# A router fed by a DMA transpose of float16 halves, with broadcast routing instructions, in a fused attention and mixture-of-experts kernel

## The chip, the cores and the metric

The program runs on one core of a Trainium2 chip. The metric is the device time of one execution in microseconds. Names of engines: PE is TensorE (PEld is its weight load), DVE is VectorE, ACT is ScalarE, POOL is GpSimd, SP is SyncE, which here only issues DMAs. "Lnnn" is a line of the kernel before, unless a text says that it is a line of the changed one.

## The reference, cut to what matters

Three layers follow one another on 2304 tokens: attention that keeps the 32 largest scores of each row, a gated two-layer network, and a mixture of eight experts in which a router picks two experts for every token.

```python
def _moe2_ref(x, w_gate, w_noise, noise, w1, w2):
    logits = x @ w_gate                                   # x: 2304 x 512, w_gate: 512 x 8
    noise_scale = np.log1p(np.exp(x @ w_noise))
    noisy_logits = logits + noise_scale * noise
    top2 = np.argpartition(-noisy_logits, 2, axis=1)[:, :2]
    top2_l = np.take_along_axis(noisy_logits, top2, axis=1)
    top2_l = top2_l - top2_l.max(-1, keepdims=True)
    top2_w = np.exp(top2_l)
    top2_w /= top2_w.sum(-1, keepdims=True) + 1e-09
    for e in range(E):
        for k in range(2):
            mask = top2[:, k] == e
            h = np.maximum(x[mask] @ w1[e], 0.0)
            out[mask] += top2_w[mask, k, None] * (h @ w2[e])
```

The router's choice is a comparison of close numbers, so its product is held to about float32. Large matmuls run on pairs of float16 numbers (a high half and the rest, a low half), as three products: high by high, high by low, low by high.

## The kernel before, in words

**The work and its stages.** Attention goes through 80 units (a pair of heads by 128 or 64 query rows). Four heads' pairs of the same rows fill a chunk of 128 or 256 tokens; there are 12 chunks, 18 tiles of 128 tokens. When a chunk is filled, `moe1` runs the gated network on it, then the router, and enters every token in the table of its two experts by an indirect DMA. When all chunks are entered, `expert` reads the tables, gathers the tokens' rows from `xd` in DRAM, turns them by a DMA transpose (L790) and runs the experts' two layers. So attention, the gated network and routing overlap from about 190 to 920 us, and experts alone follow.

**What sets the order.** Nothing is ordered by the hardware: every engine runs its instructions in the order of the program. The class `Plan` makes that order: each piece of work is an `op` with an engine, an assumed duration, a priority, the ops that it follows, an assumed delay until they see its result, and counted buffers (`alloc` takes one, the last `use` gives it back). `Plan.run` plays this through and emits every op at its turn. PE's order, DMA issues on SP, all of it comes out of that, so an edit of one op can move everything behind it. Buffers that matter here: `tp`, three PSUM banks; `y`, four SBUF tiles of 128x584 float32, used by attention's masked scores and by the router.

**The router's steps for one tile**, in `moe1`. Six ops `wo` (L573) sum the network's second layer in PSUM. `ev` on ACT copies it to `x2` (L582) and its high half to `xs` (L585). `xlo` on POOL makes the low half (L588). `xout` on SP writes both halves to `xd` (L593). Beside that, `rt` on PE turns the float32 `x2` by four transposes into a `tp` bank (L612), `re` on ACT copies that to a `y` tile (L616), and four ops `rl` multiply it with the router's weights `wr`, in float32 (L619; the profile shows two matmuls for each). For a chunk, `r1` on ACT takes exp and log (L630, L631), `r2` on DVE finds the two largest and marks them, expert by expert, one instruction for each tile and choice (L647), `r3` on PE counts the tokens ahead (L656 to L659), `r4` on DVE turns that into places, one instruction for each tile and choice (L675), and `r5` on POOL scatters (L681).

**The end.** `counts` (L844 on) counts the tokens of each expert and how many blocks overflow; a table of thresholds for it is made by an iota on POOL when it is needed (L869). In these inputs the fallback `layers(False)` and `overflow` are not run.

```python
                for kb in range(4):
                    P.transpose(q.ps[:, kb, :], ch.x2[t][:, kb * 128:(kb + 1) * 128], ident)        # rt, PE
...
                A.activation(q.xt, q.ps, AF.Copy)                                                   # re, ACT
...
                P.matmul(q.lg[:, t, 0:16], q.xt[:, kb, :], wr[:, kb, :], start=kb == 0, stop=kb == 3)  # rl, PE
```

Of the kernel before, what the change touches and what calls it, by code (L numbers as in the profile page):

```python
# [29 lines left out]
SPROD = 2.0 * SX * SV  # L30
NEG = -1.0e30
# [6 lines left out]
SW = S + 8  # L38
# [89 lines left out]
def attention_moe_kernel(ctx: ExitStack, tc: tile.TileContext, qT, kT, v, w_gate, w_val, w_out,  # L128
# [34 lines left out]
    nbi = const.tile([1, E + 2], I32, name="nbi")  # L163
    ohsum = const.tile([128, E], FH, name="ohsum")
# [15 lines left out]
    def layers(fast):  # L180
# [335 lines left out]
        def moe1(ch, prio):  # L516
# [43 lines left out]
            ch.x2, ch.hx2 = [], []  # L560
            evs = []
            for t in range(nt):
# [17 lines left out]
                def ev(r=r, t=t):  # L580
                    x2 = tile_of("x2", [128, DM], FT)
                    A.activation(x2, r.ps, AF.Copy, scale=SX2 / (SPROD * SO))  # L582
                    ch.x2.append(x2)
# [3 lines left out]
                def xlo(r=r, t=t):  # L587
                    G.tensor_tensor(r.xs[:, DM:], ch.x2[t], r.xs[:, :DM], op=OP.subtract)  # L588
# [7 lines left out]
                a = op("POOL", 1.25, prio - 1000, xlo, [evs[-1]], use=[hx, hxs])  # L596
                written.append(op("SP", 1.0, prio - 2000, xout, [a], use=[hxs], lat=3.0))
                ch.hx2.append(hx)
# [5 lines left out]
            for t in R:  # L604
                hp_, hr = plan.tile("tp"), plan.tile("y")

                def rt(t=t):
                    if t == 0:
                        q.lg = tile_of("tp", [128, nt, 32], FT)
                    q.ps = tile_of("tp", [128, 4, 128], FT)  # L610
# [3 lines left out]
                def re(t=t):  # L614
                    q.xt = tile_of("y", [128, SW], FT)[:, :512].rearrange("p (k f) -> p k f", k=4)
                    A.activation(q.xt, q.ps, AF.Copy)  # L616

                def rl(kb, t=t):
                    return lambda: P.matmul(q.lg[:, t, 0:16], q.xt[:, kb, :], wr[:, kb, :], start=kb == 0, stop=kb == 3)  # L619
                a = op("PE", 0.44, prio - 2000, rt, [evs[t]] + dep, alloc=([hl] if t == 0 else []) + [hp_], use=[ch.hx2[t]],  # L620
                       chain="moe")
                b = op("ACT", 0.5, prio - 2000, re, [a], alloc=[hr], use=[hp_])

                dep = [b]
                for kb in range(4):
                    dep = [op("PE", 0.06, prio - 2000, rl(kb), dep, use=[hr, hl], lat=0.15 if kb < 3 else None, dma=kb < 3)]
# [432 lines left out]
```

## Time and profile before

| | |
|---|---|
| median of 3 runs | 1322.95 us (1322.31 to 1325.13) |
| the profiled execution | 1323.6 us, its span 1321.9 us |
| PE busy | 1228.2 us, 93% of the span |
| PEld busy | 896.4 us, 68% |
| DVE busy | 869.1 us, 66% |
| ACT busy | 791.6 us, 60% |
| POOL busy | 740.9 us, 56% |
| mean granted clock of PE | 0.955 of 2.4 GHz |
| DMA | 119.93 MB, 91 GB/s over the span |

The shares are means over stages: weights and attention until about 190 us, attention with the gated network and routing until about 900 us, experts until the end. A busy PE is counted from the start of a matmul to its modelled end, and matmuls overlap; what one costs PE is therefore read from the distance of two starts, not from its length.

### The profile page before, as it was taken

What the parts mean: (1) busy time and instruction counts of PE and PEld (TensorE: products, weight loads), DVE (VectorE), ACT (ScalarE), POOL (GpSimd) and SP (SyncE); (2) the same over time, 40 slices, a digit from 0 to 9 for tenths busy, and PEclk for the clock granted to TensorE, in tenths of its full rate; (3) what the DMA queues carried; (4) which work ended last, traced back from release to release, by engine and by line L of the source; (5) the groups of instructions that cost most, each with busy time, mean ns of one, the idle gap of its engine ahead of it and who ended that gap; (6) DMA issues with size and microseconds to landing.
All of it is one profiled execution on the core that took longest, in us unless ns stands there. A gap on an engine that the chain in (4) does not pass through costs nothing. (4 is left out here: it accounts for less than half of the span.)

```text
span 1321.9 us, 29643 instructions
## 1 busy us (share of the span) xinstructions
PE 1228.2 (93%) x10669; PEld 896.4 (68%) x10670; DVE 869.1 (66%) x3608; ACT 791.6 (60%) x1788; POOL 740.9 (56%) x1005
## 2 busy tenths in 40 slices
PE   5578799799999999999999999999999999999997
PEld 3347466586776867886777876877666666676674
DVE  6999889998799887888789875455114324233111
ACT  5777678787777877786787774565224324333221
POOL 5989887787476786666676654442222322222221
PEclk9558899899999899999999999999999999999999
DMA  7434331342004310014100003167547576575441
GB/s 222 115 108 122 124 106 27 100 133 112 17 2 101 87 47 10 11 36 121 53 2 2 18 9 97 50 185 204 99 73 194 122 159 171 102 189 132 77 72 22
DMA packets 104463, 119.93 MB, mean 91 GB/s; under 512 B 56561, under 2 KB 65905, under 8 KB 104306
## 3 DMA queue, kind: packets, MB, share of 16 engines
q1 hardware_dynamic: 94194, 97.97, 27.1%
q0 software_dynamic: 10112, 19.97, 8.2%
q8 instruction: 86, 1.41, 0.5%
q14 instruction: 71, 0.58, 0.2%
HBM read 77.22 MB, written 20.63 MB: 74 GB/s over the span
## 5 line engine op out<-in xcount | busy, mean ns | idle before, releaser
L534 PEld LDWEIGHTS <-w 128*128 128x128 f16 x3456 | 276.9, 100 | 38.0 <-issue 12.9
L534 PE MATMUL mm<-xch,w 128*128 128x256 f16 (+1 forms) x2880 | 285.9, 256 | 7.4 <-ACT th L541 3.7
L812 DVE SCALAR_TENSOR_TENSOR g<-mm,g 128x256 f16<-128x256 f32 (+1 forms) x192 | 72.0, 379 | 243.6 <-ACT g L809 233.1
L402 POOL TENSOR_TENSOR y<-sS,sg 128x576 f32<-128x576 f32 x144 | 194.9, 1354 | 9.1
L804 PE MATMUL mm<-xch,w 128*128 128x256 f16 (+1 forms) x2016 | 190.3, 255 | 0.0
L804 PEld LDWEIGHTS <-w 128*128 128x128 f16 x2016 | 170.2, 98 | 23.5
L361 DVE MAX8 cand<-sS 128x8 f32<-128x72 f32 x1152 | 166.8, 217 | 20.6 <-ACT sS L352 20.2
L830 PEld LDWEIGHTS <-g 128*128 128x128 f16 x960 | 92.8, 98 | 106.3 <-DVE g L812 3.4
L573 PE MATMUL mm<-w,g 128*128 128x512 f16 x648 | 158.2, 389 | 1.0 <-POOL w L281 0.7
L424 DVE SCALAR_TENSOR_TENSOR e<-sS,good,e 128x576 f32<-128x576 f32 x144 | 155.5, 1099 | 2.3 <-ACT e L379 1.5
L786 POOL DMA_INDIRECT v<-xd,ids x40 | 47.0, 1175 | 163.5 <-DVE ws L776 155.1
L842 POOL DMA_INDIRECT out<-e,ids x40 | 63.8, 1595 | 131.3 <-ACT e L839 58.6
L809 ACT ACTIVATE g<-mm 128x256 f16<-128x256 f32 (+1 forms) x192 | 65.8, 346 | 112.6 <-PE mm L804 106.6
L551 POOL TENSOR_TENSOR g<-th,g 128x128 f16<-128x128 f32 (+1 forms) x144 | 93.5, 653 | 68.8 <-ACT g L548 65.7
L409 DVE MAX8 good<-y 128x8 f32<-128x584 f32 x144 | 109.9, 763 | 25.8 <-POOL y L402 21.0
L396 ACT ACTIVATE sg<-sS,m 128x576 bf16<-128x576 f32 x144 | 110.7, 770 | 23.5 <-POOL m L387 22.6
L494 PE MATMUL tp<-pt,v 128*64 128x128 f32 (+3 forms) x1600 | 116.9, 285 | 7.0 <-ACT e L379 5.1
L830 PE MATMUL tp<-w,g 128*128 128x512 f16 x504 | 115.6, 379 | 1.7 <-DVE g L812 1.6
L494 PEld LDWEIGHTS tp<-pt,v 128*64 128x64 f32 (+1 forms) x1600 | 85.2, 143 | 41.5 <-issue 23.5
L573 PEld LDWEIGHTS <-g 128*128 128x128 f16 x648 | 63.6, 100 | 67.6 <-issue 9.2
L453 PE MATMUL tp<-ident,e 128*128 128x128 f32 x576 | 91.6, 296 | 17.2 <-DVE e L424 15.7
L379 ACT ACTIVATE e<-sS,m 128x576 f32<-128x576 f32 x144 | 106.5, 768 | 0.2
(160 smaller groups left out, 2073.7 us busy)
## 6 DMA issues: line engine op xcount, KB each, us to landing
st<-w SPq DMA_DIRECT2D x64, 512.0 KB
khl<-st SPq DMA_DIRECT2D x48, 144.0 KB
st<-w_gate SPq DMA_DIRECT2D x12, 512.0 KB
st<-w_val SPq DMA_DIRECT2D x12, 512.0 KB
st<-w_out SPq DMA_DIRECT2D x12, 512.0 KB
out<-x SPq DMA_DIRECT2D x6, 768.0 KB
v<-v_s SPq DMA_DIRECT2D x16, 256.0 KB
xd<-y SPq DMA_DIRECT2D x16, 256.0 KB
```

Of the source, the lines that this page charges most:

```text
L361: V.max(T[t].cand[:, 8 * c:8 * c + 8], T[t].s[:, 72 * c:72 * c + 72])
L379: A.activation(T[t].e, T[t].s, AF.Exp, bias=T[t].m[:, CM:CM + 1], scale=SC[u.b])
L396: A.activation(T[t].sg, T[t].s, AF.Sign, scale=-CUT[0], bias=T[t].m[:, 25:26], accum_out=T[t].m[:, 26:27])
L402: G.tensor_tensor(T[t].y[:, :S], T[t].s, T[t].sg, op=OP.mult)
L409: V.max(good[:, TILES - 1 - u.i - t:TILES + 7 - u.i - t], T[t].y)
L424: return lambda: V.scalar_tensor_tensor(T[t].e, T[t].s, good[:, TILES + 6 - u.i - t:TILES + 7 - u.i - t], T[t].e, op0=OP.is_ge, op1=OP.mul ...
L494: P.matmul(u.po[64 * s:64 * s + 64, :], VB[u.b, kb][1][:k, (2 * u.hp + s) * D:(2 * u.hp + s + 1) * D], rhs, start=kb == 0, stop=kb == NK - 1)
L534: P.matmul(r.ps[:, a, :], wt.t[:, a, c, kb, fo:fo + 128], ch.x[x][:, kb, :], start=i == 0, stop=i == 11)
L551: G.tensor_tensor(r.g[:, 1], r.th, r.g[:, 0], op=OP.subtract)
L573: P.matmul(r.ps, g[:, c, 128 * t:128 * t + 128], WO[f // 4].t[:, d, f % 4, :], start=f == 0 and i == 0, stop=f == 11 and i == 2)
L804: P.matmul(r.ps, W[kb].w[c][:, 0, f * 128:f * 128 + 128], q.x[:, 4 * x + kb, :], start=i == 0, stop=i == 11)
L830: P.matmul(r.ps, gs[f].g[:, c, 128 * t:128 * t + 128], W[4 + f // 2].w[d][:, f % 2, :], start=f == 0 and i == 0, stop=f == 7 and i == 2)
```

## The change

**Router.** The float32 path (four transposes, a copy on ACT, eight float32 matmuls in the profile) goes. In its place SP issues one DMA transpose of the 128x1024 float16 tile `xs` (both halves) to a second `y` tile, and PE multiplies its eight 128x128 blocks with the router's weights, also split in two float16 halves (`wrh`, scaled by 256), in twelve float16 matmuls of 16 columns, all in one op. Exp and the logits take the scale out again. The low half now comes ahead of the router, so `xlo` gets a higher priority on POOL; `xout` is made to follow the transpose.

**Routing.** The marks of `r2` become one broadcast comparison for a chunk, the places of `r4` one broadcast product and one reduction for a chunk.

**Counts.** The table of thresholds becomes a constant, made at the start; the priority of `counts` goes from PX to PX + 3000 (a larger number is later).

```diff
+SR = 2.0 ** 8
+    steps = const.tile([1, E, NB], FT, name="steps")
+    G.iota(steps, pattern=[[0, E], [BLK, NB]], base=CAP, ...)
+    wrh = const.tile([128, 2, 4, 16], FH, name="wrh")
...
-                a = op("POOL", 1.25, prio - 1000, xlo, [evs[-1]], use=[hx, hxs])
-                written.append(op("SP", 1.0, prio - 2000, xout, [a], use=[hxs], lat=3.0))
+                a = op("POOL", 1.25, prio - 2000, xlo, [evs[-1]], use=[hx, hxs])
+                hr = plan.tile("y")
+                def xturn(r=r):
+                    r.xt = tile_of("y", [128, SW], FT).bitcast(FH)[:, :2 * DM].rearrange("p (k f) -> p k f", k=8)
+                    nc.sync.dma_start_transpose(r.xt, r.xs)
+                r.turned = op("SP", 1.35, prio - 2000, xturn, [a], alloc=[hr], use=[hxs], lat=3.0)
+                written.append(op("SP", 1.0, prio - 2000, xout, [r.turned], use=[hxs], lat=3.0))
...
                 for kb in range(4):
-                        P.transpose(q.ps[:, kb, :], ch.x2[t][:, kb * 128:(kb + 1) * 128], ident)
-                    A.activation(q.xt, q.ps, AF.Copy)
-                    return lambda: P.matmul(q.lg[:, t, 0:16], q.xt[:, kb, :], wr[:, kb, :], start=kb == 0, stop=kb == 3)
+                        for i, (c, d) in enumerate(((0, 0), (0, 1), (1, 0))):
+                            P.matmul(q.lg[:, t], ch.x2[t].xt[:, 4 * c + kb, :], wrh[:, d, kb, :],
+                                     start=kb == 0 and i == 0, stop=kb == 3 and i == 2)
+                dep = [op("PE", 0.8, prio - 2000, rt, [ch.x2[t].turned] + dep, alloc=[hl] if t == 0 else [],
+                          use=[ch.x2[t].hr] + ([hl] if t else []), chain="moe")]
...
-                for t in R:
-                    for k in range(2):
-                        V.tensor_scalar(q.oh[:, t, k], iota8, xf[:, t, k:k + 1], None, op0=OP.is_equal)
+                V.tensor_tensor(q.oh, iota8[:, None, None, :].to_broadcast([128, nt, 2, E]),
+                                xf[:, :, :, None].to_broadcast([128, nt, 2, E]), op=OP.is_equal)
...
-                    for k in range(2):
-                        V.scalar_tensor_tensor(jk, q.oh[:, t, k], 1.0, q.ns[:, t], op0=OP.mult, op1=OP.mult,
-                                               accum_out=slf[:, t, k:k + 1])
+                V.tensor_tensor(q.oh, q.oh, q.ns[:, :, None, :].to_broadcast([128, nt, 2, E]), op=OP.mult)
+                V.tensor_reduce(slf, q.oh, axis=mybir.AxisListType.X, op=OP.add)
...
-                G.iota(thr, pattern=[[0, E], [BLK, NB]], base=CAP, ...)
-            a = op("PE", 0.2, PX, total, [a] + routers[-1:], alloc=[hp], chain="moe")
+            a = op("PE", 0.2, PX + 3000, total, [a] + routers[-1:], alloc=[hp], chain="moe")
...
-            op("POOL", 0.2, 26, lambda: G.tensor_scalar(wr, wr, 1.0 / SX2, 1.0, op0=OP.mult, op1=OP.mult), [a])
+                G.tensor_scalar(wr, wr, SR, 1.0, op0=OP.mult, op1=OP.mult)
+                G.tensor_copy(wrh[:, 0], wr)
+                G.tensor_tensor(wrh[:, 1], wr, wrh[:, 0], op=OP.subtract)
+            op("POOL", 0.6, 26, split_router, [a])
```

The order on the engines moves as follows. In these rows a line of the changed kernel is a few higher or lower than its counterpart: L621 is the router's float16 matmul, L605 the transpose, L597 `xout`; L348, L457, L475, L477, L498 are L344, L453, L471, L473, L494 of before; L538 and L577 are L534 and L573, L799 and L825 are L804 and L830, L710 is L715 (a load of expert weights), L785 is L790.

First, PE behind the third chunk (its tiles 2 and 3, the first chunk of 256 tokens), before:

```order
L573 MATMUL mm<-w,g 128x512
L612 MATMUL tp<-ident,x_4645 128x128 x4
L494 MATMUL tp<-pt,v 64x128 x10
L344 LDWEIGHTS qs
L344 MATMUL ps<-khl,qs 128x288
...
L453 MATMUL tp<-ident,e 128x128 x4
L619 MATMUL tp<-wr,y 128x16 x2
L453 MATMUL tp<-ident,e 128x128 x4
L619 MATMUL tp<-wr,y 128x16 x2
```

and now, from the last `wo` matmul on:

```order
L577 MATMUL mm<-w,g 128x512
L457 MATMUL tp<-ident,e 128x128 x8
...
L475 MATMUL tp<-ident,px 128x128
L477 MATMUL tp<-ident,e 64x128 x2
...
L498 MATMUL tp<-pt,v 64x128 x10
L457 MATMUL tp<-ident,e 128x128 x8
...
L621 LDWEIGHTS y
L621 MATMUL tp<-wrh,y 128x16
...
L475 MATMUL tp<-ident,px 128x128
L477 MATMUL tp<-ident,e 64x128 x2
```

Left out of the second piece are four score matmuls (L348) at each of its first three gaps and the rest of the twelve router matmuls at the last; twelve more follow behind its end, those of tile 3. The four transposes are gone, and the router's matmuls stand together, behind attention's work.

Second, PE at the last tile (17), now:

```order
L577 MATMUL mm<-w,g 128x512
L799 LDWEIGHTS khl
L799 MATMUL mm<-xch,khl 128x256
...
L825 LDWEIGHTS g
L825 MATMUL tp<-khl,g 128x512
...
L621 LDWEIGHTS y
L621 MATMUL tp<-wrh,y 128x16
```

Left out are repetitions: there are 72 matmuls of L799, 6 of L825 and 12 of L621. In the kernel before the transposes of this tile stood behind 36 matmuls of L804 and 6 of L573, and its router matmuls were spread over the next 72 of L804 and L830.

Third, SP's issues at that tile (with the semaphores that a row waits for), before:

```order
L790 DMA_TRANSPOSE xch<-v 128x8x128 [waits DMASW4_49,PE_49]
L715 DMA st<-w 128x2x512 [waits DMAHW6_49,DVE_49]
L593 DMA xd<-y 128x1024 [waits DMASW5_49,Pool_49]
L790 DMA_TRANSPOSE xch<-v 128x8x128
L715 DMA st<-w 128x2x512 [waits DMAHW7_49,DMAHW5_49,DVE_49]
```

and now:

```order
L710 DMA st<-w 128x2x512 [waits DMAHW4_49,DVE_49]
L785 DMA_TRANSPOSE xch<-v 128x8x128 [waits DMASW4_49,PE_49]
L785 DMA_TRANSPOSE xch<-v 128x8x128 [waits DMASW5_49]
L605 DMA_TRANSPOSE y<-y 128x8x128 [waits Pool_49]
L597 DMA xd<-y 128x1024
L710 DMA st<-w 128x2x512 [waits DMAHW6_49,DMAHW5_49,DVE_49]
```

The router's transpose stands behind both of an expert's transposes, each of which waits for a gather (DMASW), and `xout` stands behind the router's.

## Rows read from the trace of the kernel before

**Rows 1.** Windows: window, length, busy (count) by engine, PEclk, DMA share, GB/s
```profile
300.00:900.00 600.00, 583.90 (x5687) 451.40 (x5686) 474.01 (x2279) 437.83 (x1033) 383.31 (x602) 0.99 0.19 54
...
200.00:300.00 100.00, 86.24 (x789) 66.14 (x788) 96.06 (x442) 78.88 (x184) 80.58 (x117) 0.93 0.34 96
...
400.00:500.00 100.00, 93.93 (x839) 70.40 (x837) 88.33 (x412) 76.39 (x175) 76.62 (x112) 0.97 0.30 78
500.00:600.00 100.00, 99.62 (x1046) 80.67 (x1044) 82.99 (x437) 78.37 (x192) 65.41 (x108) 1.00 0.10 25
...
900.00:1000.00 100.00, 99.91 (x780) 67.88 (x779) 30.68 (x96) 31.82 (x69) 27.68 (x23) 1.00 0.55 114
```
**Rows 2.** Timeline of PE at tile 16: start, length, engine, line, op, operands, count
```profile
864.21 0.61 PE L612 MATMUL tp<-ident,x 128*128 128x128 f32 x4
864.65 2.84 PE L534 MATMUL mm<-xch,w 128*128 128x128 f16 x48
867.33 0.35 PE L619 MATMUL tp<-wr,y 128*128 128x16 f32 x2
867.53 0.83 PE L534 MATMUL mm<-xch,w 128*128 128x128 f16 x12
```
**Rows 3.** Timeline of PE: the small float16 matmuls of r3
```profile
364.11 0.17 PE L656 MATMUL tp<-both,tri 128*128 128x8 f16 x1
...
364.24 0.60 PE L534 MATMUL mm<-xch,w 128*128 128x256 f16 x4
```
**Rows 4.** Groups by line and form: busy us, mean ns, idle before it
```profile
L612 PEld LDWEIGHTS tp<-ident,x 128*128 128x128 f32 x72 | 8.3, 146 | 1.5 <-ACT x L582 0.8 <-ACT px L480 0.4
L619 PEld LDWEIGHTS tp<-wr,y 128*128 128x128 f32 x144 | 22.2, 198 | 3.6 <-ACT y L616 1.8 <-issue 0.9 <-ACT g L548 0.2
L616 ACT ACTIVATE y<-tp 128x512 f32<-128x512 f32 x18 | 10.7, 592 | 1.1 <-PE tp L612 1.1
L647 DVE TENSOR_SCALAR oh<-iota,xf 128x8 f32<-128x8 f32 x36 | 6.3, 235 | 0.4
L675 DVE SCALAR_TENSOR_TENSOR jk<-oh,ns 128x8 f32<-128x8 f32 x36 | 9.9, 274 | 0.6
```
**Rows 5.** Timeline of tile 13 (PE, ACT, POOL): from its last wo matmul to the low half
```profile
766.28 2.75 PE L573 MATMUL mm<-w,g 128*128 128x512 f16 x12
...
769.49 0.57 ACT L582 ACTIVATE x<-mm 128x512 f32<-128x512 f32 x1
...
772.64 1.16 POOL L588 TENSOR_TENSOR y<-x,y 128x512 f16<-128x512 f32 x1
```
**Rows 6.** Timeline of SP: the last expert transpose, and the issues at tile 17
```profile
1276.15 1.23 SPq L790 DMA_TRANSPOSE xch<-v  x1
...
898.70 0.34 SPq L593 DMA_DIRECT2D xd<-y  x1
```
**Rows 7.** Windows around that last transpose: its packets (columns as in rows 1)
```profile
1278.50:1279.00 0.50, 0.50 (x5) 0.20 (x2) 0.00 (x0) 0.00 (x0) 0.43 (x1) 1.00 0.30 65
1279.00:1279.50 0.50, 0.50 (x4) 0.26 (x3) 0.00 (x0) 0.00 (x0) 0.00 (x0) 1.00 0.00 0
```
**Rows 8.** The gathers of 128 rows (L786), all 40 of them
```profile
DMA to landing us min/median/max: 3.3/3.7/7.6
```
**Rows 9.** Timeline of PE: the last wo matmuls of tile 17
```profile
891.13 1.46 PE L573 MATMUL mm<-w,g 128*128 128x512 f16 x6
```
**Rows 10.** Timeline of PE between 502 and 508 us: what attention's pieces cost
```profile
502.84 1.46 PE L494 MATMUL tp<-pt,v 128*64 128x128 f32 x20
504.23 1.09 PE L453 MATMUL tp<-ident,e 128*128 128x128 f32 x8
505.16 0.65 PE L344 MATMUL ps<-khl,qs 128*128 128x288 f16 x4
505.65 1.47 PE L534 MATMUL mm<-xch,w 128*128 128x256 f16 x12
506.96 0.27 PE L471 MATMUL tp<-ident,px 128*128 128x128 f32 x1
```

More of the change, by code (lines that the diff above doesn't have):

```diff
@@ L604, in moe1 @@
             for t in R:
-                hp_, hr = plan.tile("tp"), plan.tile("y")
                 def rt(t=t):
                     if t == 0:
-                        q.lg = tile_of("tp", [128, nt, 32], FT)
-                    q.ps = tile_of("tp", [128, 4, 128], FT)
+                        q.lg = tile_of("tp", [128, nt, 16], FT)
                     for kb in range(4):
-                        P.transpose(q.ps[:, kb, :], ch.x2[t][:, kb * 128:(kb + 1) * 128], ident)
-                def re(t=t):
-                    q.xt = tile_of("y", [128, SW], FT)[:, :512].rearrange("p (k f) -> p k f", k=4)
-                    A.activation(q.xt, q.ps, AF.Copy)
-                def rl(kb, t=t):
-                    return lambda: P.matmul(q.lg[:, t, 0:16], q.xt[:, kb, :], wr[:, kb, :], start=kb == 0, stop=kb == 3)
[L620 to L626, printed above, removed]
+                        for i, (c, d) in enumerate(((0, 0), (0, 1), (1, 0))):
[3 more added lines that the diff above has]
+                          use=[ch.x2[t].hr] + ([hl] if t else []), chain="moe")]
             def r1():
                 q.sp = small.tile([128, nt, E], FT, name="sp", bufs=2)
-                A.activation(q.sp, q.lg[:, :, 8:16], AF.Exp)
+                A.activation(q.sp, q.lg[:, :, 8:16], AF.Exp, scale=1.0 / (SR * SX2))
                 A.activation(q.sp, q.sp, AF.Ln, bias=one_c)
@@ L664, in r4 @@
                 q.sl = small.tile([128, nt, 2], I32, name="sl", bufs=4)
-                jk = small.tile([128, E], FT, name="jk", bufs=1)
                 V.tensor_scalar(q.dd[:, :, 0], q.dd[:, :, 1], 1.0, 1e-9, op0=OP.add, op1=OP.add)
@@ L684, in moe1 @@
             a = op("ACT", 1.6, prio - 2000, r1, dep, use=[hl])
-            b = op("DVE", 2.0, prio - 2000, r2, [a], use=[hl])
+            b = op("DVE", 1.7, prio - 2000, r2, [a], use=[hl])
             c = op("ACT", 0.25, prio - 2000, lambda: A.activation(q.dd[:, :, 1], q.dd[:, :, 0], AF.Exp), [b])
@@ L688, in moe1 @@
             d = op("PE", 0.2, prio - 2000, r3, [b] + routers[-1:], alloc=[hpp], chain="moe")
-            e = op("DVE", 1.65, prio - 2000, r4, [c, d], use=[hpp])
+            e = op("DVE", 1.5, prio - 2000, r4, [c, d], use=[hpp])
             for t in R:
@@ L881, in counts @@
             hy = plan.tile("y")
-            a = op("DVE", 0.3, PX, settled, ranks, alloc=[hy]) if fast else None
-            a = op("PE", 0.2, PX, total, [a] + routers[-1:], alloc=[hp], chain="moe")
-            op("DVE", 2.5, PX, blocks, [a], alloc=[] if fast else [hy], use=[hp, hy] if fast else [hp])
+            a = op("DVE", 0.3, PX + 3000, settled, ranks, alloc=[hy]) if fast else None
+            a = op("PE", 0.2, PX + 3000, total, [a] + routers[-1:], alloc=[hp], chain="moe")
+            op("DVE", 2.5, PX + 3000, blocks, [a], alloc=[] if fast else [hy], use=[hp, hy] if fast else [hp])
         units = []
```

16 lines of the change are left out of this document (9 added, 7 removed).

## The prediction

> **What bounds the kernel now.** Three views, in this order. First the windows of 100 us: from 400 on PE is busy for 93.9 to 99.9 us of each 100, at a granted clock of 0.97 to 1.00, that is at 2.4 GHz nearly throughout, while DVE, the next, has 83 to 88 us in attention's stretches and 31 us in the experts' [rows 1]. From 200 to 300 it is the other way round: DVE 96.1 us, PE 86.2 [rows 1]. So what PE no longer has to do is worth its time from about 300 on, and little ahead of that. Second, the timeline of PE at a router, where the reader is to read starts, not lengths: what an instruction costs PE is the time until the next one starts. Third, the timeline of ACT, POOL and SP from the last `wo` matmul of a tile to `xout`, since the changed router hangs on that chain and not on `x2` any more.
>
> **The change part by part.**
>
> *PE loses the float32 router.* At tile 16 the four transposes start at 864.21 and the next matmul at 864.65: 0.44 us. A pair of router matmuls starts at 867.33 and the next at 867.53: 0.20 us, four times: 0.80 us [rows 2]. So 1.24 us for a tile, 22.3 us for all 18.
>
> *PE gains twelve float16 matmuls of 16 columns for a tile*, each with 128x128 weights of its own. Not one of that form is in the trace. From below, the router's counting matmuls (8 columns, 128x128 weights that change each time): five of them start from 364.11 to 364.24, 26 ns each [rows 3]. From above, the gated network's matmuls of 128 columns, also with new weights each: 48 from 864.65 to the next start at 867.33, 56 ns each [rows 2]. I take 26, since 16 columns are far nearer to 8 than to 128: 0.31 us for a tile, 5.6 us for all; from above 0.67 and 12.1.
> The Trainium skill (TensorE: Matmul & The Clock Gate, "Wait — 56ns, not 53.3ns?") gives two floors for small matmuls, about 25 ns from start to start, and about 62 ns of sequencer work for each where decoding is done in microcode; by the second the twelve would cost an estimated 0.74 us and all of them 13.4. The row of five at 26 ns speaks for the first.
>
> *The difference*: 22.3 - 5.6 = 16.7 us, 0.93 us for a tile. Two tiles lie ahead of 300 us, where PE is not the bound; I count them at nothing, their cover being DVE's 96 us [rows 1]. If that cover is not there they give 1.9 us more. Sixteen tiles: **-14.8 us**. From above (56 ns) it is 16 x (1.24 - 0.67) = -9.1.
>
> *Waits removed.* PE's weight load sat idle for 1.5 us ahead of the transposes and 3.6 us ahead of the router's matmuls [rows 4]. The order around them is made anew, so I take 0 of these 5.1 us and keep -5.1 as the end.
>
> *Waits added.* The router now waits for `ev`, `xlo` and a transpose. At tile 13 the last `wo` matmul ends at 769.03, ACT starts to copy at 769.49, POOL starts the low half at 772.64 and ends at 773.80: 4.8 us [rows 5]. A transpose of this very form issued with little else in flight at 1276.15 has its last packets in the half microsecond from 1278.50 [rows 6, 7]: 2.4 to 2.9 us, I take 2.6. Beside weight loads it can be later; the nearest rows are gathers of as many bytes, 3.3 to 7.6 us to landing [rows 8]. So the chain is 7.4 us, at most 4.8 + 7.6 = 12.4. `xlo`'s higher priority shortens it, which I don't count.
> What covers it is PE's work that stands, in the new order, between a chunk's last `wo` matmul and its last router. For tile 3: two groups of eight transposes (L457, 0.93 us each: 504.23 to 505.16), three of four score matmuls (0.49 each), two `px` groups (some 0.33), one L498 (1.39) and the other tile's router (0.31): 5.7 us [rows 10]. For tile 17: 72 matmuls of 256 columns at 0.109 (twelve in 1.31) and 6 of 512 at about 0.22: 9.2 us [rows 10]. Counted so, the twelve chunks have 15.4, 2.9, 5.7, 8.6, 10.0, 10.2, 10.1, 10.6, 9.2, 9.9, 7.4 and 9.2 us. Against 7.4, tile 3 waits 1.7 us. The second chunk, at 220 us, is short by 4.5, but there the planner had nothing else for PE; I count that as hidden beside DVE, and 4.5 if it isn't. At tile 17 SP is late too: before, the issue of `xout` came at 898.70, behind a wait for a gather; the transpose now stands behind one more expert transpose of 1.23 us [rows 6], so its data come at about 898.7 + 1.3 + 2.6 = 902.6, against a cover that ends at 892.59 + 9.2 = 901.8 [rows 9]: 0.8 us, and up to 3 beside the weight loads. I take 1.8. Together **+3.5 us**. A PE that waits holds up everything behind the router, experts' matmuls included.
>
> *Other engines.* ACT loses the copy, 10.7 us [rows 4]; at 76 to 78 us busy of 100 [rows 1] that is off the path, and if ACT were the bound it would be more gain. DVE loses 36 marks (6.3 us) and 36 places (9.9) [rows 4] and gets 36 instructions for chunks; at the 235 ns of the marks, 8.5 us. Some 8 us less, hidden by PE. SP issues 18 more DMAs of 1.23 us, 22 us in all; what stands behind them is `xout`, now 1.3 us later, and loads that come tens of us early; covered as long as SP is idle between chunks. POOL gets two small instructions at the start and the constant; it is not the bound at any time [rows 1]. The counts come later, in the experts' stretch where PE has 99.9 us of 100 and DVE 31 [rows 1]: nothing.
>
> **The sum.** 1323.6 (the profiled execution, 1321.9 of it its span) - 14.8 + 3.5 = 1312.3. That execution is 0.65 us above the median of the runs shown, so **1311.6 us** for a median.
>
> **What is not in the sum.** Plan re-makes the order of every engine behind the first router. In rows the size of that luck is PE's idle time in one stretch of attention: 6.1 us in the worst, 0.4 in the best [rows 1]. Six such stretches lie between 300 and 900. If they differ at random by a third of that span, some 2 us each, that is about 5 us in all, either way.
>
> **The rivals.**
>
> *PE waits for the transpose (slower).* The place is the router op in PE's order. At a chain of 10.5 us the ten chunks from the third on would wait 14 us together (10.5 less each cover), and the gain is gone: that is the point from which it decides. At 12 us they wait 29.1, which gives 1323.0 + 29.1 - 14.8 = 1337. For it: a gather took up to 7.6 us [rows 8], SP's queue holds an issue behind any wait [rows 6]. Against it: the DMA engines are little used in such a stretch (a share of 0.10 from 500 to 600), and 10.5 would need some 6 us for each transpose [rows 1, 7]. The Trainium skill speaks for this rival (VectorE: DVE Perf Modes, "The three transpose paths" and its rules): a DMA transpose of 128x128 is put at 1309 ns against 390 on TensorE, with the advice to take TensorE wherever PSUM will do as destination. Chance 0.09.
>
> *Attention is paced by its chain, not by PE.* Then PE's saved time turns into waits until attention ends, and only the last four tiles give something: 4 x 0.93 = 3.7, given back by the added waits of 3.5: 1322.8, no change. For it: DVE's 83 to 88 us. Against it: PE's 99.6 us in 500 to 600 [rows 1]. Chance 0.10.
>
> *The small matmuls cost 56 ns, as those of 128 columns do.* Then 16 tiles give 9.1 us: 1323.0 - 9.1 + 3.5 = 1317. For it: the weights are as large as there [rows 2]. Against it: so they are in r3, at 26 ns [rows 3]. Chance 0.10.
>
> *The new order is the worse one.* Every stretch of attention idles as the worst does, 6 x 6.1 = 36.6 us where PE is idle for 16 from 300 to 900 now [rows 1]: +20.5 - 11.3, 1332. Chance 0.05.
>
> **How the numbers follow.** My forecast has 0.66, with a range of its own from 1303 (removed waits gone, no added ones, a little luck) to 1318. A measurement of this kernel can tell about 0.2%, 2.6 us, from no change. Faster by more: the forecast, the third rival and a part of the second, 0.80. Within: most of the second and the milder cases of the first, 0.09. Slower: the rest of the first, the last, and a tail, 0.11. The range of 8 in 10 is 1302 to 1322: the lower end takes -14.8 - 5.1 and 1 us of luck, the upper reaches the second rival.
>
> **What the profile after would show.** Right: no L612 and L616; the router's twelve matmuls in one block of 0.3 to 0.4 us; PE busy for some 15 us less, with the stretches from 300 to 900 just as full, and attention's end earlier by 10 us; a transpose issued right behind each low half. Wrong: idle time on PE of over 2 us ahead of the router line at most chunks (the first rival); idle time ahead of attention's transposes grown by about 10 us (the second); a block of 0.7 us or more (the third).

## The result, and the profile after

The changed kernel takes 1331.81 us (median of 6 runs, 1328.24 to 1335.04); the kernel before, run beside it on the same chip, 1325.15. The ratio is **1.0052** with a 95% interval of 1.003 to 1.0073: slower by half a per cent, about 7 us. The prediction said 1311.6, in a range of 1302 to 1322. The time lies where the last rival put it (1332, chance 0.05); how far its reason holds is said further down.

The page of the changed kernel, busy time of each engine (share of the span, instructions):

```profile
span 1330.0 us, 29534 instructions
...
PE 1213.5 (91%) x10669; PEld 877.6 (66%) x10670; DVE 858.7 (65%) x3536; ACT 784.5 (59%) x1770; POOL 748.3 (56%) x1007
```

PE is busy for 14.7 us less than before, DVE for 10.4 less, ACT for 7.1 less. Only POOL, busy for 56%, has 7.4 us more. PE, DVE and ACT have less to do, and the span is 8.1 us longer, so the loss is idle time in the main. The granted clock is no worse over the whole span, 0.977 in the mean against 0.955 before; it is worse in one stretch, between 219 and 342 us, as shown below.

The windows of the changed kernel (window, length, busy and count of PE, PEld, DVE, ACT, POOL, granted clock, DMA share, GB/s), to be held against [rows 1]:

```profile
200.00:300.00 100.00, 81.04 (x741) 60.17 (x742) 84.35 (x408) 74.45 (x172) 76.86 (x112) 0.88 0.37 105
...
300.00:900.00 600.00, 573.52 (x5693) 437.64 (x5691) 469.41 (x2242) 431.80 (x1021) 390.15 (x605) 0.99 0.22 58
...
900.00:1000.00 100.00, 96.34 (x767) 65.70 (x765) 28.65 (x89) 30.38 (x65) 25.30 (x19) 1.00 0.56 118
```

Read them by what is missing to the full length. From 300 to 900 PE idles for 26.5 us instead of 16.1. From 200 to 300 DVE, which had 96.1 us there, has 84.4, and PE 81.0 instead of 86.2. From 900 to 1000, where PE had 99.91, it has 96.34. No stretch has the whole loss.

The router itself does what was forecast. PE at tiles 2 and 3 (start, length, engine, line, operands, count):

```profile
355.67 0.45 PE L621 MATMUL tp<-wrh,y 128*128 128x16 f16 x12
355.98 0.31 PE L475 MATMUL tp<-ident,px 128*128 128x128 f32 x1
356.12 0.38 PE L477 MATMUL tp<-ident,e 128*64 128x128 f32 x2
356.34 0.45 PE L621 MATMUL tp<-wrh,y 128*128 128x16 f16 x12
356.64 1.58 PE L538 MATMUL mm<-xch,w 128*128 128x256 f16 x13
```

From start to next start a block of twelve costs 0.31 and 0.30 us, 26 ns for one, as in [rows 3]. And it hardly waits. Who waited for whom at that line, over all 18 tiles (us, times, longest), for PE and for its weight load:

```profile
PE tp L621 <- DMA y<-y: 1.9, 2, 1.5
PE tp L621 <- DVE cand L374: 0.9, 1, 0.9
PEld L621 <- DMA y<-y: 4.0, 3, 2.0
```

The weight load's 4.0 us are not added to PE's: its waits include the same three moments. So PE idles for 1.9 us for the transposes, and at most 0.9 more at the one place where a result of DVE came last.

**Work and stalls of PE.** To part the two, every matmul is given the median distance from its start to the next start, over all matmuls of its kind in all the traces here. The sum of these is PE's work; what remains until the last matmul is stall. Only differences between kernels are to be read: attention's `pt` matmuls (L498) are followed either after some 7 ns or after 50 to 200, about as often, so that their median, and with it the work of every kernel, can move by tens of us with the way of counting. Stall holds idle time and also the time by which PE is slower than usual. The last three columns split it; they are of one profiled execution each, and the times of the changed kernel alone scatter by 7 us.

| kernel | work, us | stalls, us | third stretch of attention (some 219 to 342 us) | the other nine to the last `wo` | experts |
|---|---|---|---|---|---|
| before | 1152.8 | 159.9 | 25.3 | 47.7 | 2.4 |
| changed | 1134.4 | 186.1 | 32.2 | 62.6 | 8.0 |

The rest of the stalls, 84.5 and 83.3 us, lies in the first two chunks' stretches. Work fell by 18.4 us, stalls grew by 26.2: 6.9 in the third stretch, 14.9 in the other nine, 5.6 in the experts. The last `wo` matmul comes at 894.0 us instead of 892.2, so 18 us of saved work brought attention's end no nearer.

What PE waited for in the other nine stretches (342 to 885 us; us, times, longest), before:

```profile
PE tp L453 <- DVE e L424: 0.6, 1, 0.6
PE mm L534 <- DVE th L544: 0.4, 1, 0.4
```

and in the changed kernel:

```profile
PE tp L457 <- DVE e L428: 5.9, 6, 2.2
PE mm L538 <- DVE th L548: 4.3, 5, 1.5
PE mm L577 <- DVE th L548: 2.8, 2, 2.4
```

So there PE waits for results of DVE, of attention (`e`) and of the gated network (`th`), though DVE has not more to do. The third stretch is another matter. Its windows, before and after:

```profile
219.00:342.00 123.00, 109.96 (x988) 82.38 (x986) 110.72 (x526) 96.98 (x226) 94.11 (x142) 0.96 0.34 100
219.00:342.00 123.00, 105.90 (x922) 77.47 (x921) 101.70 (x500) 90.57 (x212) 87.67 (x136) 0.90 0.35 102
```

PE idles for 4.1 us more, and the granted clock is 0.90 instead of 0.96: of its two levels, 1.2 and 2.4 GHz, PE had the lower for an estimated 25 us there instead of 10 (worked out from these two means). So 4.1 of the 6.9 us are idle time, and the rest goes with the slower clock. It fell to 0.50 at 225 us, after 5 us in which PE was busy for 2.0 (changed kernel):

```profile
220.00:225.00 5.00, 2.01 (x16) 1.03 (x12) 2.47 (x4) 2.72 (x6) 4.69 (x7) 0.96 0.00 0
225.00:230.00 5.00, 2.57 (x20) 1.83 (x20) 3.11 (x14) 3.73 (x8) 3.69 (x7) 0.50 0.42 105
```

### The profile page after: what moved, and what is told of

Its sections match the earlier page's. It is cut to its first block, busy times and chain, and to the rows that moved or that the text cites. A ratio compares the mean times of both kernels' runs of the same rounds, so it can differ in the third digit from the quotient of the medians.

```text
span 1330.0 us, 29534 instructions
## 1 busy us (share of the span) xinstructions
PE 1213.5 (91%) x10669; PEld 877.6 (66%) x10670; DVE 858.7 (65%) x3536; ACT 784.5 (59%) x1770; POOL 748.3 (56%) x1007
## 5 line engine op out<-in xcount | busy, mean ns | idle before, releaser
L538 PEld LDWEIGHTS <-w 128*128 128x128 f16 x3456 | 272.0, 99 | 39.8 <-issue 16.7
L538 PE MATMUL mm<-xch,w 128*128 128x256 f16 (+1 forms) x2880 | 278.8, 254 | 9.0 <-DVE th L548 6.5
L807 DVE SCALAR_TENSOR_TENSOR g<-mm,g 128x256 f16<-128x256 f32 (+1 forms) x192 | 71.9, 379 | 235.4 <-ACT g L804 228.6
L799 PE MATMUL mm<-xch,w 128*128 128x256 f16 (+1 forms) x2016 | 190.3, 255 | 0.0
L799 PEld LDWEIGHTS <-w 128*128 128x128 f16 x2016 | 170.2, 98 | 23.4
L825 PEld LDWEIGHTS <-g 128*128 128x128 f16 x960 | 92.9, 98 | 107.2 <-DVE g L807 3.1
L577 PE MATMUL mm<-w,g 128*128 128x512 f16 x648 | 157.8, 387 | 4.7 <-DVE th L548 2.8
L428 DVE SCALAR_TENSOR_TENSOR e<-sS,good,e 128x576 f32<-128x576 f32 x144 | 149.1, 1056 | 6.1 <-ACT e L383 5.0
L804 ACT ACTIVATE g<-mm 128x256 f16<-128x256 f32 (+1 forms) x192 | 66.2, 346 | 117.7 <-PE mm L799 108.8
L555 POOL TENSOR_TENSOR g<-th,g 128x128 f16<-128x128 f32 (+1 forms) x144 | 97.7, 682 | 54.7 <-ACT g L552 53.5
L413 DVE MAX8 good<-y 128x8 f32<-128x584 f32 x144 | 109.9, 763 | 25.0 <-POOL y L406 20.5
L498 PE MATMUL tp<-pt,v 128*64 128x128 f32 (+3 forms) x1600 | 117.9, 286 | 1.2 <-ACT pt L482 1.2
L825 PE MATMUL tp<-w,g 128*128 128x512 f16 x504 | 115.5, 379 | 2.3 <-DVE g L807 1.6
L457 PE MATMUL tp<-ident,e 128*128 128x128 f32 x576 | 91.4, 297 | 25.7 <-DVE e L428 24.2
L498 PEld LDWEIGHTS tp<-pt,v 128*64 128x64 f32 (+1 forms) x1600 | 86.0, 144 | 38.1 <-issue 23.8
L577 PEld LDWEIGHTS <-g 128*128 128x128 f16 x648 | 63.3, 100 | 70.7 <-issue 13.1
```

What stands on the lines that cost most here:

```text
L413: V.max(good[:, TILES - 1 - u.i - t:TILES + 7 - u.i - t], T[t].y)
L428: return lambda: V.scalar_tensor_tensor(T[t].e, T[t].s, good[:, TILES + 6 - u.i - t:TILES + 7 - u.i - t], T[t].e, op0=OP.is_ge, op1=OP.mul ...
L498: P.matmul(u.po[64 * s:64 * s + 64, :], VB[u.b, kb][1][:k, (2 * u.hp + s) * D:(2 * u.hp + s + 1) * D], rhs, start=kb == 0, stop=kb == NK - 1)
L538: P.matmul(r.ps[:, a, :], wt.t[:, a, c, kb, fo:fo + 128], ch.x[x][:, kb, :], start=i == 0, stop=i == 11)
L555: G.tensor_tensor(r.g[:, 1], r.th, r.g[:, 0], op=OP.subtract)
L577: P.matmul(r.ps, g[:, c, 128 * t:128 * t + 128], WO[f // 4].t[:, d, f % 4, :], start=f == 0 and i == 0, stop=f == 11 and i == 2)
```

## The experiments

Four theories. **The order** (O in the expectations)**:** what was lost is the difference between two orders that `Plan` makes, and the change's instructions are a gain when the order is held. **The waits:** the router's wait for its transpose holds up PE. **The second tile:** the `y` tile that the transposed data take is missing to attention (Y). **The assumed costs:** `Plan` is told that the new router costs PE 0.8 us and that its data come 1.35 + 3.0 us after the low half, where the trace has 0.31 and 2.4 to 2.9 us behind the issue; it then puts other things in the way (C).

### One half of the change at a time

`turn_only` has the router by DMA transpose, with marks, places, table and counts as before. Its edit, against the changed kernel:

```diff
-                V.tensor_tensor(q.oh, iota8[:, None, None, :].to_broadcast([128, nt, 2, E]), ...)
+                for t in R:
+                    for k in range(2):
+                        V.tensor_scalar(q.oh[:, t, k], iota8, xf[:, t, k:k + 1], None, op0=OP.is_equal)
...
-            b = op("DVE", 1.7, prio - 2000, r2, [a], use=[hl])
+            b = op("DVE", 2.0, prio - 2000, r2, [a], use=[hl])
```

> The router by DMA transpose alone; marks, places and counts as before. PE's own work should fall by some 17 to 18 us in every theory. If the loss is the new order that Plan makes (theory O), the time may come out anywhere between 1318 and 1334 us and need not lie near the sum of the parts. If it is the second y tile that a router tile now holds (theory Y), it is as slow as the whole change, 1329 to 1333. If the experts' stretch lost its 6 us by the later counts, this kernel has them back: about 1325.

Measured: 1337.68 us, ratio **1.0084** (1.0063 to 1.0106), slower than any theory had it.

`routing_only` is the other half: broadcast marks and places, the constant table, later counts, with the router of before. Its edit, against the changed kernel again:

```diff
-                dep = [op("PE", 0.8, prio - 2000, rt, [ch.x2[t].turned] + dep, ...)]
+                a = op("PE", 0.44, prio - 2000, rt, [evs[t]] + dep, ...)
+                b = op("ACT", 0.5, prio - 2000, re, [a], alloc=[hr], use=[hp_])
```

> Broadcast marks and places, the constant table and the later counts, with the router as before. Theory Y expects no loss: 1320 to 1325 us, DVE some 8 us less busy and PE as before. Theory O expects a shift of either sign of up to 6 us, since Plan's order is made anew here too. If the later counts cost the experts' stretch, it is 5 us longer there.

Measured: 1334.01 us, **1.0066** (1.0041 to 1.0092). Each half alone is slower than before, so the two do not add: their sum would be 1.5%, and both together cost 0.5. The routing half leaves PE's work where it was (1152.8), and its instructions on DVE are some 10 us shorter; that this costs 9 us, more than the 6 that theory O had expected at most, can't come from its instructions, unless the new ones are bad in a way that the trace hides. The next run settles that.

### The same instructions in the order of before

`routing_same_plan` has the new marks, places and table, but the assumed durations and priorities of before, so that every engine keeps its order. Against the kernel before:

```diff
-                for t in R:
-                    for k in range(2):
-                        V.tensor_scalar(q.oh[:, t, k], iota8, xf[:, t, k:k + 1], None, op0=OP.is_equal)
+                V.tensor_tensor(q.oh, iota8[:, None, None, :].to_broadcast([128, nt, 2, E]),
+                                xf[:, :, :, None].to_broadcast([128, nt, 2, E]), op=OP.is_equal)
...
             b = op("DVE", 2.0, prio - 2000, r2, [a], use=[hl])
```

> Broadcast marks and places and the constant table, with the plan of the kernel before (durations and the counts' priority not changed), so that the order of every engine is the old one. Theory O expects no loss: 1322 to 1327 us against 1325.6, unlike the same instructions in their own plan, which were 0.66% slower. If those instructions themselves cost, 1330 or more.

Measured: 1323.8 us, **1.0001** (0.9987 to 1.0014). From this to `routing_only` nothing but two assumed durations and the priority of the counts differs: 0.65%. The windows from 200 to 300, first of `routing_only`:

```profile
200.00:300.00 100.00, 80.60 (x719) 59.29 (x721) 84.20 (x407) 72.73 (x171) 77.65 (x111) 0.93 0.36 99
```

and of `routing_same_plan`:

```profile
200.00:300.00 100.00, 86.60 (x799) 65.65 (x797) 95.08 (x445) 80.33 (x188) 82.07 (x120) 0.95 0.36 100
```

With the order of before, DVE is at 95 again; re-made, it has the 84 of the changed kernel. The granted clock is nearly the same in both, 0.93 and 0.95. So for these instructions the loss of the third stretch comes with the new order alone.

`all_same_plan` has all of the change's instructions in the order of before: `rt`, `re` and three of the four `rl` stay as ops, but issue nothing of the old router; the last `rl` issues the twelve matmuls, and `xout` issues the transpose, into `x2`'s own buffer. Against the kernel before:

```diff
                 def xout(r=r, t=t):
+                    xt = r.x2.bitcast(FH).rearrange("p (k f) -> p k f", k=8)
+                    nc.sync.dma_start_transpose(xt, r.xs)
+                    ch.xt[t] = xt
...
-                    return lambda: P.matmul(q.lg[:, t, 0:16], q.xt[:, kb, :], wr[:, kb, :], start=kb == 0, stop=kb == 3)
+                        if kb < 3:
+                            return
+                        for j in range(4):
+                            for i, (c, d) in enumerate(((0, 0), (0, 1), (1, 0))):
+                                P.matmul(q.lg[:, t, 0:16], ch.xt[t][:, 4 * c + j, :], wrh[:, d, j, :], ...)
```

> The whole change in instructions, with the plan of the kernel before: Plan is given the old ops, durations and buffers, so every engine keeps its old order; the twelve matmuls stand where the last float32 router matmul stood, the transpose right ahead of the issue that writes xd, and its data go into the x2 buffer. Theory O (the new order took the gain and more) expects PE's 16 to 18 us nearly whole: 1308 to 1314 us. If the transpose itself is what costs (PE waits for it, or it holds up SP), 1322 us or more, with idle time ahead of the router's line on PE.

Measured: 1316.49 us, **0.9945** (0.9928 to 0.9963): faster than before and than the changed kernel, by instructions that are those of the change. Between it and the changed kernel lie 1.1%, some 14 us, for the order and the buffer that goes with it. That buffer by itself is no gain in a re-made order, as `x2_tile` below shows (1340.74 us). It gains 7 us and not 18; 1308 to 1314 us were expected. What holds the other 11 is shown in part: its stalls in the experts are 9.2 us (before, 2.4), and PE idles at the router. PE's weight load and PE at the router of tile 4, with the idle time ahead in brackets:

```profile
433.32 0.40 PEld L628 LDWEIGHTS <-x 128*128 128x128 f16 x12 [4.47 <-DMA x<-y]
433.32 0.49 PE L628 MATMUL tp<-wrh,x 128*128 128x16 f16 x12 [4.24 <-ACT pt L464]
```

The copy on ACT that ended PE's wait:

```profile
432.75 0.58 ACT L464 ACTIVATE pt<-tp 128x512 f32<-128x512 f32 x1
```

The first transpose on SP ahead of that:

```profile
429.97 1.85 SPq L597 DMA_TRANSPOSE x<-y  x1
```

And PE's waits at the router line in all (us, times, longest):

```profile
PE tp L628 <- ACT pt L464: 4.2, 1, 4.2
PE tp L628 <- DMA x<-y: 1.7, 1, 1.7
```

The transpose is issued 3.3 us ahead of the matmuls, and its data and the end of ACT's copy (432.75 + 0.58 = 433.33) come together: with an earlier transpose PE would still have waited for ACT. So of the 6.0 us that PE idles at its router, 1.7 are the transpose's alone. That is the first rival's wait, at a fraction of its price.

### How far one order lies from another

`before_p82` and `before_p78` are the kernel before with one assumed duration, of a small copy on ACT in attention, 10 ns longer and 10 ns shorter. Not one instruction is another; their order is, from 283 us on in `before_p78` and from 508 us on in `before_p82`. Ahead of that they have the order of the kernel before.

```diff
-            d = op("ACT", 0.16, prio - 1, xh, [a], use=[hpx, ch.h])
+            d = op("ACT", 0.17, prio - 1, xh, [a], use=[hpx, ch.h])
```

> The kernel before, instruction for instruction, with one assumed duration of Plan off by 0.01 us (the high half of attention's output on ACT, 0.17 for 0.16). Theory O expects a shift of several us of either sign, up to 0.6%. If the order is not that sensitive, within 0.2% of the kernel before.

> The kernel before with the assumed duration of attention's high half at 0.15 us instead of 0.16: a third sample of how far Plan's order moves the time with no instruction changed. With 0.17 it was 0.32% slower. I expect 1322 to 1332; if the order before was simply a lucky one, slower than before again.

Measured: 1328.65 us, **1.0032** (1.0022 to 1.0043), and 1339.59 us, **1.0116** (1.0101 to 1.0131). The second loses 15 us by a number that describes nothing new; at most 1332 us were expected. Its windows, 300 to 900 and the rest:

```profile
300.00:900.00 600.00, 577.24 (x5602) 445.85 (x5601) 466.61 (x2268) 430.99 (x1020) 376.89 (x599) 0.99 0.17 50
...
900.00:1336.00 436.00, 420.96 (x3273) 287.62 (x3270) 129.59 (x310) 139.53 (x284) 109.90 (x81) 0.99 0.54 121
```

Behind 300 us it is the changed kernel's picture without the change: 22.8 us idle from 300 to 900, and 15 of 436 in the experts, where the kernel before idles for 10.9 of 422 (PE busy 411.09 from 900 to 1322).

The same for the changed kernel, `after_p82` and `after_p78`:

> The changed kernel with the same assumed duration off by 0.01 us. Theory O expects a shift of several us against the changed kernel, so between 1325 and 1340. Otherwise 1330 to 1333.

> The changed kernel with the assumed duration of attention's high half at 0.15 us instead of 0.16: a third order for the same instructions. If the order decides, it may lie anywhere from 1322 to 1342 and shows how wide the draw is; if the change itself costs the time, 1330 to 1334 again.

Measured: 1334.01 us, **1.0072** (1.0048 to 1.0095), and 1331.65 us, **1.0046** (1.0031 to 1.0062). These two moved by 0.2% or less, no more than was expected if the order hardly mattered. So three orders of the kernel before have 1.000, 1.0032 and 1.0116, three of the changed one 1.0046, 1.0052 and 1.0072. The means are 1.0049 and 1.0057. The kernel before is the luckiest of its three; the changed kernel is an ordinary one of its own. But luck is not all: between the means PE's 18 us of saved work (1.4%) are missing as well. The changed kernel's three orders are the same up to some 300 us, too, so none of the six draws the whole third stretch anew.

From 300 to 860 us the idle time of PE shows more than luck. The windows of `before_p78`, the changed kernel and `true_costs` (further down):

```profile
300.00:860.00 560.00, 544.97 (x5248) 419.16 (x5247) 445.48 (x2219) 408.73 (x975) 359.82 (x580) 0.99 0.14 42
300.00:860.00 560.00, 540.28 (x5303) 411.83 (x5302) 448.66 (x2195) 408.33 (x972) 372.61 (x585) 0.99 0.20 49
300.00:860.00 560.00, 545.45 (x5406) 417.31 (x5404) 443.03 (x2186) 410.60 (x984) 368.59 (x590) 1.00 0.19 51
```

In four orders with the old router (`before`, `before_p78`, `before_p82`, `routing_only`) PE idles there for 13.6 to 15.4 us; in five with the new router at its assumed costs (the changed kernel, `after_p78`, `after_p82`, `x2_tile`, `turn_only`) for 19.6 to 22.0, with no overlap; in the one order with corrected costs for 14.6. (`all_same_plan`, in the order of before, has 16.8.) Some 6 us of the loss are therefore common to all orders that `Plan` made for the new router at those costs.

### What is PE's time worth?

`double_router` is the kernel before with the float32 router matmuls of every tile issued twice, in the same order.

```diff
+                        for j in range(4 if kb == 3 else 0):
+                            P.matmul(q.lg[:, t, 0:16], q.xt[:, j, :], wr[:, j, :], start=j == 0, stop=j == 3)
```

> The kernel before in its own order, where the float32 router matmuls of each tile are done a second time behind the first (the same sums again), which is 18 x 0.8 = 14 us more work on PE and nothing else. If PE's work from 300 us on is worth its time, as the prediction took it, 1335 to 1339 us (some 13 us more). If attention's chain hides it, 1325 to 1330.

Measured: 1339.86 us, **1.011** (1.0089 to 1.0131): +15 us for some 14 us of added work (0.80 us for each of 18 tiles, [rows 2]). With the order held, work added to PE costs its time. This speaks against the second rival, that attention is paced by something else. Work taken away was worth 7 of 18 us in a held order (`all_same_plan`).

### The second tile

`x2_tile` puts the transposed data in an `x2` buffer, so that attention keeps all four `y` tiles.

```diff
-                hr = plan.tile("y")
+                hr = plan.tile("x2")
```

> The whole change, with the transposed tile in an x2 buffer, which the router no longer needs, in place of a y buffer. Theory Y expects most of the stalls back: PE's waits in attention fall by 10 us or more, 1315 to 1322 us. Theory O expects no system in it: between 1324 and 1335. It still reads and writes the same data.

Measured: 1340.74 us, **1.0107** (1.0079 to 1.0135), with 195.8 us of stalls, slower than either theory had it. Nothing for theory Y; but the edit re-makes the order as well, and a difference of this size is within what an order does, so it can't be ruled out either.

### The assumed costs

`true_costs` is the changed kernel with the router's assumed costs nearer to the measured ones.

```diff
-                r.turned = op("SP", 1.35, prio - 2000, xturn, [a], alloc=[hr], use=[hxs], lat=3.0)
+                r.turned = op("SP", 1.25, prio - 2000, xturn, [a], alloc=[hr], use=[hxs], lat=1.5)
...
-                dep = [op("PE", 0.8, prio - 2000, rt, ...)]
+                dep = [op("PE", 0.3, prio - 2000, rt, ...)]
```

> The whole change, with the costs that Plan assumes for the new ops set to what the trace shows: 0.3 us for the twelve matmuls (0.8 assumed), 1.25 + 1.5 us for the transpose (1.35 + 3.0 assumed). Theory C (Plan lays out its order for a slower router, and the holes stay) expects 8 us or more of gain over the changed kernel, 1316 to 1323 us. Theory Y expects 2 to 4 us of gain, as y tiles are held a little shorter in the plan. Theory O expects any shift of up to 6 us.

Measured: 1321.27 us, **0.9975** (0.9961 to 0.9988), with the change's instructions, as theory C expected (1316 to 1323). Stalls are 179.4 instead of 186.1 us, the third stretch's still 34.2.

### The last tile, behind the gathers

At tile 17 SP's queue decides. Its issues in the changed kernel:

```profile
899.93 3.59 SPq L785 DMA_TRANSPOSE xch<-v  x2
903.57 1.33 SPq L605 DMA_TRANSPOSE y<-y  x1
904.94 0.58 SPq L597 DMA_DIRECT2D xd<-y  x1
905.63 13.46 SPq L710 DMA_DIRECT2D st<-w  x7
...
925.88 0.33 SPq L767 DMA_DIRECT2D tb<-tab  x1
```

PE at the router of that tile and at the wait that follows, in the changed kernel:

```profile
906.71 0.46 PE L621 MATMUL tp<-wrh,y 128*128 128x16 f16 x12 [1.53 <-DMA y<-y]
...
928.29 2.78 PE L799 MATMUL mm<-xch,khl 128*128 128x256 f16 x24 [1.51 <-DVE g L807]
```

And DVE just ahead of the second:

```profile
927.69 0.15 DVE L770 CAST ids<-tb 128x1 int32<-128x1 f32 x1 [3.96 <-DMA tb<-tab]
927.82 1.08 DVE L807 SCALAR_TENSOR_TENSOR g<-mm,g 128x256 f16<-128x256 f32 x3
```

The router's transpose comes behind two expert transposes (3.59 us in SP's queue, the second waiting for a gather), and PE waits 1.53 us at 906.71. Later the table load (L767) stands behind seven weight loads, the conversion that needs it (L770) waits 3.96 us at the head of DVE's queue, and with it L807 and PE.

`after_gather6` tells `Plan` that the first expert's gathers take longer, which lets the router's transpose go first. Its order is that of the changed kernel up to about 870 us.

```diff
-                c = op("POOL", 1.1, prio - 2000, gather, [b], alloc=[hv], use=[ht], lat=2.5)
+                c = op("POOL", 1.1, prio - 2000, gather, [b], alloc=[hv], use=[ht], lat=2.5 if e else 6.0)
```

> The changed kernel, with 6.0 us instead of 2.5 assumed in Plan for the landing of the first expert's gathers. Up to about 860 us every order is the changed kernel's; behind it the last tile's transpose stands ahead of an expert's pair of transposes on SP, not behind it. If the late transpose of that tile is what made the experts' stretch longer, PE's stalls behind the last wo matmul fall from 8 us to 4 or less, and the time by 3 to 6 us, to some 1327 (ratio to before about 1.002). If not, 1330 or more.

Measured: 1327.85 us, **1.0026** (1.0012 to 1.004). Its issue on SP:

```profile
898.42 1.23 SPq L605 DMA_TRANSPOSE y<-y  x1
```

And PE at the router:

```profile
903.16 0.45 PE L621 MATMUL tp<-wrh,y 128*128 128x16 f16 x12
```

The transpose is issued 5.2 us earlier and the wait is gone; the experts' stalls go from 8.0 to 6.0 us, and 4 or less were expected. The table load is still late (issued at 922.93 us; at 925.88 in the changed kernel, at 920.20 in the kernel before), so that wait does not come from the late transpose. The conversion that waits for it, first in `after_gather6`, then in the kernel before:

```profile
924.62 0.15 DVE L770 CAST ids<-tb 128x1 int32<-128x1 f32 x1 [4.46 <-DMA tb<-tab]
921.91 0.15 DVE L775 CAST ids<-tb 128x1 int32<-128x1 f32 x1 [2.29 <-DMA tb<-tab]
```

In `after_gather6` PE then waits 2.00 us for DVE at 925.22; in the kernel before it does not wait there. The intervals of 1.0026 and 1.0052 overlap, so half of the loss lying here is likely, not shown.

The same edit on the two fastest kernels, `true_gather6` and `same_gather6`:

> Both corrections of Plan's assumptions: the router's new ops at their measured costs, and 6.0 us for the first expert's gathers. If both mechanisms are right and add up, 1315 to 1319 us, the ratio to before 0.993 to 0.996. If order is mere luck, anywhere from 1316 to 1332.

> The change's instructions in the order of the kernel before, but with 6.0 us assumed for the first expert's gathers, so that the order is the old one up to about 860 us. If the late last transpose is the loss in the experts' stretch, its 9 us of stalls there fall to 4 or less: 1311 to 1314 us, the ratio 0.990 to 0.993. If not, 1316 or more.

Measured: 1319.64 us, **0.9962** (0.9948 to 0.9976), and 1318.78 us, **0.9963** (0.995 to 0.9976). The first lies 0.13% below `true_costs`, within the intervals; the two have one order up to some 866 us, and on PE throughout. Both were expected lower (1315 to 1319, 1311 to 1314). The second is a clear miss: 0.9945 became 0.9963, no gain, and within the intervals no loss either, while the experts' stalls fell from 9.2 to 4.5 us in the profiled executions. The windows of `true_gather6`:

```profile
300.00:900.00 600.00, 581.17 (x5778) 445.29 (x5779) 469.03 (x2239) 438.19 (x1034) 384.16 (x605) 0.99 0.24 64
...
900.00:1000.00 100.00, 99.27 (x783) 68.16 (x781) 28.61 (x83) 30.30 (x65) 29.48 (x22) 1.00 0.53 107
```

It is as full from 300 to 900 as the kernel before within 3 us, and nearly as full from 900 to 1000, on 18.4 us less work. That is near the profile which the forecast expected of the changed kernel.

## Why the prediction was wrong

**PE's work: right.** -16.7 us forecast, 18.4 found. Twelve matmuls take 0.31 us, and the third rival, 56 ns for each, falls with that. The Trainium skill (TensorE: Matmul & The Clock Gate, "Wait — 56ns, not 53.3ns?") gives a floor of 25 ns from start to start. The 26 ns of the trace agree with it; its 62 ns do not show here.

**That PE's time is worth its length: right for work that is added, half right for work that is taken away.** In a fixed order `double_router` gives +15 for +14 us, `all_same_plan` -7 for -18.

**The waits: right kind, size a little high.** Forecast 3.5 us, found 1.9 at the router for the transposes, and 0.9 where DVE came last together with one. Tile 17's data were forecast for 902.6 us and came by about 906.7, since both expert transposes stand ahead and one waits for its gather; PE's wait there is 1.5 us, 1.8 were forecast. Not forecast was the table load, late in both kernels, on which PE waits in the changed one. The first rival is out: its 14 to 29 us are 1.9. The advice of the Trainium skill that spoke for it (VectorE: DVE Perf Modes, "The three transpose paths": TensorE where PSUM will do) does not decide here. In the changed kernel waits of 1.9 us for the transposes stand against 18.4 us of PE's work. The 5.1 us of removed waits that the lower end took were the weight load's; PE itself idled for only 1.6 us at the old router (1.3 for L616, 0.3 for L582).

**The other engines: right that they count nothing.** DVE's 36 new instructions take 12 x (184 + 177 + 178) ns = 6.5 us (forecast 8.5, before 16.2), and `routing_same_plan` shows their worth: 1.0001.

**A sign of the second rival came nearly true.** It was to be idle time ahead of attention's transposes, grown by about 10 us. The groups of these transposes (busy us, mean ns, idle before, and what ended it), before, in the changed kernel and in `all_same_plan`:

```profile
L453 PE MATMUL tp<-ident,e 128*128 128x128 f32 x576 | 91.6, 296 | 17.2 <-DVE e L424 15.7 <-ACT y L280 1.2
L457 PE MATMUL tp<-ident,e 128*128 128x128 f32 x576 | 91.4, 297 | 25.7 <-DVE e L428 24.2
L457 PE MATMUL tp<-ident,e 128*128 128x128 f32 x576 | 90.5, 295 | 16.7 <-DVE e L428 15.7
```

It grew by 8.5 us in the changed kernel, and not at all in the order of before. So it comes with the new order, and not because attention's chain paced PE all along.

**The step that failed is "What is not in the sum".** The re-made order was put at about 5 us either way, from the idle time of six stretches taken as independent and with no bias. The runs show 14 us between two orders of the change's own instructions (and two homes of the transposed data), and 0 to +15 us for the kernel before, by a change of 10 ns in one assumed duration. Three things were overlooked. The kernel before was one draw of its kind and, of the three seen here, the fastest, so a new draw was likely to lose (by 4 and 15 us). There is a bias besides: from 300 to 860 us every order made for the new router at its assumed costs leaves PE idle for some 6 us more. And only the stretches from 300 to 900 were counted; the third stretch gave away 6.9 us, part of it by a lower clock, and the experts 5.6, where a late load on SP's queue still stops PE. So the fourth rival, at 1332 and 0.05, has the right kind of cause, but that its time is met to the microsecond is partly chance: it laid 20.5 us of new idle time between 300 and 900, where 10.4 are found, and the rest of the loss lies in other places.

**What stays open.** Why `Plan` makes the worse orders: corrected costs end the bias of some 6 us, but that is one order (`true_costs` and `true_gather6` share it), 0.9975 and 0.9962 against 1.0026 to 1.0107 for the six kernels with the assumed costs of the change. And which re-ordering costs the third stretch its 6 to 9 us: every kernel has it whose ops were changed (30.9 to 34.2, `routing_only` among them), none that keeps the ops of before (24.0 to 25.6). Those others all have the order of before in most or all of that stretch, `before_p78` up to 283 us; so it may be no more than that this one order was a good one there.

## What to carry to other kernels

Where a planner makes the order, an edit has two effects: of its instructions, and of a new draw. Price the first by holding the order (emit the new instructions from the old ops), and the second by shifting one assumed duration a little, in both kernels, several times; if that spread is larger than the gain, then no single pair of times says anything of the edit. Look where the orders part: what lies ahead of that is the same draw. When a view of a wait is read, keep PE and its weight load apart, or the same wait is counted twice. Give the planner measured costs for a new op, and look in each DMA queue for what stands ahead of a transfer that the busiest engine will now wait for.

## What the runs showed that was not expected

- An assumed duration of 0.15 in place of 0.16 us, with the same instructions, makes the program 15 us slower (1.0116). The whole redesigned router gains 7 us in a held order.
- A broadcast comparison of 128x16 or 128x32 elements takes 174 to 194 ns, less than the 235 ns of one mark of 128x8 that takes its other operand per partition [rows 4]. The new marks in the changed kernel, from the view of their line (ns minimum/median/maximum, first and last start, forms):

```profile
L643 DVE TENSOR_TENSOR oh<-iota,xf x12: 174/184/194, 207.4 to 910.2; 128x16 f32<-128x16 f32 x6, 128x32 f32<-128x32 f32 x6
```
